# Start of the program, x transfers and idle matmuls re-ordered in a convolution and ELU-MLP kernel

## Chip, core and metric

The kernel runs on one core of a Trainium2 chip. The metric is device time in microseconds from one launch. Five engines work on their own instruction streams and meet only at semaphores: TensorE (PE; its weight loads are listed apart as PEld), VectorE (DVE), ScalarE (ACT), GpSimd (POOL) and SyncE (SP). SP, ACT and POOL also issue transfers (DMA). TensorE writes to PSUM, which here is split into a ring of three slots `H` and an accumulator `ops`.

## What is computed

The reference cut to what matters (x has 8 batches of 4096 rows of 192 channels, `weight` is 8 heads by 7 taps, `w_in` is 192 by 2048, `w_out` is 2048 by 192):

```python
w = softmax(weight, axis=-1)                      # one 7-tap filter for each head
x_pad = concat([zeros(B, 6, D), x], axis=1)       # six zero rows ahead of every batch
out[b, s, h] = sum_k w[h, k] * x_pad[b, s + k, h] # causal convolution, 24 channels a head
h = out.reshape(32768, 192) @ w_in
g = where(h > 0, h, exp(min(h, 0)) - 1)
result = g @ w_out
```

## The kernel before

**Tiling.** The 32768 rows are cut into 32 supers of 1024 rows; four supers make a batch. The 2048 hidden columns are cut into 16 pairs, each 128 columns by 1024 rows (two halves of 512). So the program has 512 pairs. A list called `order`, made ahead of the program, gives the sequence that PE, ACT and SP follow: convolution halves `("c", m)`, pairs `("h", n)` and pieces of the output product `("o", t, half, r0, r1)`.

**A pair.** PE makes the hidden values of a pair in one slot of H with six matmuls (L494). ACT takes the exponential of each half into a buffer `E` (L372), POOL clamps it to at most 1 (L308), and DVE forms max(h, e - 1) from E and from the same slot of H into `gT` (L421). Only when DVE is done is the slot free. There are three slots in turn, so a pair's matmuls wait for DVE's work on the pair three slots back (`wait_slot`, L441); a convolution half takes a slot as well. The output product of super t (L523) reads `gT` and runs on PE between the pairs of super t+1, and one piece of it ahead of that, behind pair 15 of super t. `ops` is copied out by ACT (L346) twice a super.

**The convolution.** It is a matmul of x (stationary, 24 channels of one head) with a band matrix that holds the seven taps on its diagonals (L472), 40 matmuls for half a super. The result goes through ACT (L361) to `csb`, by SP to a buffer in DRAM (`conv_slots`, L569) and back into `att` in another layout (L241). In super s the second half of the convolution of super s+1 comes behind pair 4, the first half of super s+2 behind pair 12 (`CONV_AT`).

**x.** POOL issues the loads of x for super s+2 between its clamps of super s (`X_AT`, `load_x`): at step 2 only for the first super of a batch (a small memset of the six zero rows, L257, and a transfer of the rest of window 0, L258), at step 4 windows up to 4 (L271), at step 12 windows 5 to 8 (L271). A load waits until the convolution of super s no longer needs the buffer (`s_cv`), and a step's load stands in POOL's stream ahead of that step's clamps.

**The start.** DVE makes the filter weights. SP writes a zeroed tile Tm to DRAM (`conv_band`, L544), writes the taps over its diagonal (L555), and reads the band back as `Tk`, taps and heads interleaved, heads innermost (L557). DVE and ACT each copy one half of the heads of Tk into `Tm`, which has columns innermost (L407, L326). PE runs 34 idle matmuls on a zero tile (L453, `WARM`), then the two convolution halves of super 0 out of Tm, then 24 idle matmuls, then pair 0. The second half of the convolution of super 0 is copied out by DVE (L411). POOL loads x of super 0 first, waits for the taps in DRAM (`s_band` at 32, L287), loads the first 1024 columns of w_in (L276), copies these to the upper 64 partitions (L291), waits for both convolution halves (L292), loads x of super 1, waits for `att` of super 0 (L295), and loads the other columns of w_in. w_out is loaded at step 8 of super 0 (L300).

Of the kernel before, what the change touches and what calls it, by code (L numbers as in the profile page):

```python
# [12 lines left out]
P = 128  # L13
# [3 lines left out]
HEADS = 8  # L17
# [4 lines left out]
CW = 122  # L22
# [6 lines left out]
NG3 = 2  # L29
LAG = -1  # L30
QA = 8
WARM = (34, 24)
HALF_STEPS = (10, 10, 6, 6, 10, 11, 11)

CONV_AT = ((4, 1, 1), (12, 2, 0))
EARLY_CONV = {1: (1, 0), 4: (1, 1), 12: (2, 0)}
XW = 5
X_AT = ((2, 0), (4, 1), (12, 2))
W_OUT_AT = 8

PIECES = (
# [6 lines left out]
def bass_lightweight_conv__then__act_elu_kernel(  # L48
# [84 lines left out]
    with ExitStack() as stack:  # L133
# [73 lines left out]
        NDMA_ATT = 6  # L207
        x_need, z_need, x_count, z_count = {}, {}, [0] * NXB, 0
        for s in range(NS):
            x_count[s % NXB] += 16 + 16 * (s % SPB == 0)  # L210
            z_count += s % SPB == 0
            x_need[s, 0] = x_count[s % NXB]
            x_need[s, 1] = 16 * (s // NXB + 1)
            z_need[s] = z_count
# [30 lines left out]
        @block.gpsimd  # L245
        def _gpsimd(g: bass.BassGpSimd):
            W = Waits(g)

            def load_x(s, part):
                b, t0 = s % NXB, s * SUP  # L250
                first = s % SPB == 0
                if part == 0 and not first:
                    return
                if s >= NXB:
                    W(s_cv, 2 * (s - NXB) + 2)
                if part == 0:
                    g.memset(xg[0:PAD, b, 0, :], 0.0).then_inc(s_z)  # L257
                    g.dma_start(  # L258
                        xg[PAD:P, b, 0, :], x_flat[t0 : t0 + P - PAD, :]
                    ).then_inc(s_x[b][0], 16)  # L260
                    return
                if part == 1:
                    w0, w1, row = int(first), XW, t0 - PAD + CW * first
                else:
                    w0, w1, row = XW, NWIN, t0 + SUP - P - CW * (NWIN - 1 - XW)
                src = bass.AP(
                    tensor=x_flat.tensor,
                    offset=row * D,
                    ap=[[D, P], [CW * D, w1 - w0], [1, D]],
                )  # L270
                g.dma_start(xg[:, b, w0:w1, :], src).then_inc(s_x[b][part - 1], 16)  # L271

            def load_w_in(k):
                c0, c1 = WCOLS[k]
                for j in range(3):
                    g.dma_start(  # L276
                        w_in[0:HP, j, c0:c1],
                        bass.AP(
                            tensor=moe_w_in.tensor,
                            offset=8 * j * FF + c0,  # L280
                            ap=[[CPH * FF, HEADS], [FF, 8], [1, c1 - c0]],
                        ),
                    ).then_inc(s_w[k], 16)

            for part in range(3):
                load_x(0, part)
            W(s_band, 32)  # L287
            load_w_in(0)
            W(s_w[0], 48)
            c0, c1 = WCOLS[0]  # L290
            g.dma_start(w_in[HP:P, :, c0:c1], w_in[0:HP, :, c0:c1]).then_inc(s_wdp, 16)  # L291
            W(s_cv, 2)  # L292
            for part in range(3):
                load_x(1, part)
            W(s_att[0], 16 * NDMA_ATT)  # L295
            load_w_in(1)
            for n in range(NP):
                s, i = divmod(n, NQ)
                if n == W_OUT_AT:
                    g.dma_start(  # L300
                        w_out[:, :, :], moe_w_out.rearrange("(q p) d -> p q d", p=FC)
                    ).then_inc(s_w[2], 16)
                for at, part in X_AT:
                    if at == i and s + NXB < NS:
                        load_x(s + NXB, part)
                for u in range(2):
                    W(s_exp, 2 * n + u + 1)
                    g.tensor_scalar(  # L308
                        out=E[:, n % NE, u, :],
                        in0=E[:, n % NE, u, :],  # L310
                        scalar1=1.0,
                        scalar2=0.0,
                        op0=ALU.min,
                        op1=ALU.max,
                    ).then_inc(s_clp)

        @block.scalar
        def _scalar(a):
            W = Waits(a)
            a.memzero(scr[:, 0:1]).then_inc(s_scr)  # L320
            W(s_scr, 1)
            a.activation(scr[:, 1:2], scr[:, 0:1], ACT.Exp)
            W(s_set, 2)
            a.activation(wex[:], wq2[:], ACT.Exp).then_inc(s_wex)
            W(s_band, 48)
            a.activation(  # L326
                Tm[:, HEADS // 2 :, :].rearrange("p h t -> p t h"),
                Tk[:, :, HEADS // 2 :],
                ACT.Copy,
            ).then_inc(s_tm)  # L330

            def evac(t, half):
                n_half = 2 * t + half
                W(s_mm2, n_half + 1)
                b = n_half % 2
                W(s_out[b], 32 * (n_half // 2))
                if (t, half) == last_half:
                    a.activation(  # L338
                        osb[:, b, 0, :, :].rearrange("p k d -> p (k d)"),
                        H[:, last_slot % 3, 0 : 2 * D],  # L340
                        ACT.Copy,
                    ).then_inc(s_oev)
                    W(s_od, 1)
                    out_group(a, t, half, 1)
                    return
                a.activation(  # L346
                    osb[:, b, :, :, :].rearrange("p g k d -> p g (k d)"),
                    ops[:, :, 0 : 2 * D],
                    ACT.Copy,
                ).then_inc(s_oev)  # L350

            for item in order:
                if item[0] == "c":
                    m = item[1]
                    if m == 1:
                        W(s_dw[0], 16)
                        read_att(a, W, 0, 0)
                        continue
                    W(s_cv, m + 1)
                    W(s_dw[m % 4], 16 * (m // 4))  # L360
                    a.activation(  # L361
                        csb[:, m % 4, :, :],
                        H[:, slot_of_conv[m] % 3, :].rearrange("p (b t) -> p b t", b=2),
                        ACT.Copy,
                    ).then_inc(s_ce)
                elif item[0] == "h":
                    n = item[1]
                    k = slot_of_pair[n] % 3
                    W(s_h, n + 1)
                    W(s_tt, 2 * (n - NE) + 2)  # L370
                    for u in range(2):
                        a.activation(  # L372
                            E[:, n % NE, u, :], H[:, k, GS * u : GS * (u + 1)], ACT.Exp
                        ).then_inc(s_exp)
                else:
                    _, t, half, r0, r1 = item
                    if r1 == NR:
                        evac(t, half)

        @block.vector  # L380
        def _vector(v):
# [21 lines left out]
                ALU.mult,  # L403
            ).then_inc(s_set)
            v.memset(H[:, 0:2, :], 0.0).then_inc(s_hz)
            W(s_band, 48)
            v.tensor_copy(  # L407
                Tm[:, 0 : HEADS // 2, :].rearrange("p h t -> p t h"), Tk[:, :, 0 : HEADS // 2]
            ).then_inc(s_tm)
            W(s_cv, 2)  # L410
            v.tensor_copy(  # L411
                csb[:, 1, :, :],
                H[:, slot_of_conv[1] % 3, :].rearrange("p (b t) -> p b t", b=2),
            ).then_inc(s_cd)
            for n in range(NP):
                s, q = divmod(n, NQ)
                if s >= NG3:
# [20 lines left out]
        def _tensor(pe):  # L438
# [17 lines left out]
            for item in order:  # L456
                if item[0] == "c":
                    m = item[1]
                    s, g = divmod(m, 2)
                    if m == 0:  # L460
                        W(s_tm, 2)
                        W(s_hz, 1)
                    for part in range(g + 1):
                        W(s_x[s % NXB][part], x_need[s, part])
                    W(s_z, z_need[s])
# [2 lines left out]
                    for hb in range(2):  # L468
                        for (w, c0, nc_, o) in PIECES[g]:
                            for q in range(4):  # L470
                                h = 4 * hb + q
                                ins = pe.matmul(  # L472
                                    H[SLOT * q : SLOT * q + CPH, k % 3,
                                      GS * hb + o : GS * hb + o + nc_],
                                    xg[:, s % NXB, w, CPH * h : CPH * (h + 1)],
                                    Tm[:, h, PAD + c0 : PAD + c0 + nc_],
                                    start=True,
                                    stop=True,
                                    tile_position=(0, SLOT * q),
                                )  # L480
                    ins.then_inc(s_cv)
                elif item[0] == "h":
                    n = item[1]
                    s, q = divmod(n, NQ)
                    if n == 0:
                        warm(WARM[1])
                    W(s_w[q // QA], 48)
                    W(s_wdp if q < QA else s_wd[1], 16)
                    W(s_att[s % 2], 16 * NDMA_ATT * (s // 2 + 1))
# [131 lines left out]
```

## Time and profile before

| what | value |
|---|---|
| median of 3 runs | 786.17 us (785.61 to 786.69) |
| the profiled execution | 785.69 us |
| its span, first to last instruction | 783.9 us |
| PE, POOL, ACT, DVE busy | 96%, 85%, 84%, 81% of the span |
| first matmul of pair 0 | at 28.12 us |
| first pair of super 1 | at 55.45 us |
| last instruction of L421 (DVE) ends | at 771.4 us |

The times in the profile are microseconds from the start of the span. A busy PE in the table is not a PE at its peak, since a matmul's end is modelled. In a timeline row stand start, length, engine, line, operation, destination and source, the number of instructions merged (x6), and in brackets the idle time ahead of it with the name of what ended it. A row of windows gives for a stretch its length, then busy time and number of instructions of PE, PEld, DVE, ACT and POOL, the granted clock of TensorE, the share of the DMA engines in use, and the rate.

### The profile page before, as it was taken

To read this page: it belongs to the slowest core of one execution; us is meant where nothing else is said; L and a number is where in the kernel's file an instruction comes from. 1 tells how busy PE (TensorE), PEld (TensorE's weight loads), DVE (VectorE), ACT (ScalarE), POOL (GpSimd) and SP (SyncE) were. 2 spreads that over 40 slices of the span, in tenths; PEclk is the share of its full clock that TensorE was granted. 3 is DMA by queue.
4 is the path that set the end of the run, shared out by engine and by line. 5 is a ranking of instruction groups with operands and counts; after the bars stand their busy time and mean duration, and the time that the engine had idled before them with its cause. 6 is when DMAs were issued, how large, how long until landed. Compare 5 with 4: busy or idle time off the path is not lost.

```text
span 783.9 us, 32275 instructions
## 1 busy us (share of the span) xinstructions
PE 751.1 (96%) x13882; PEld 514.9 (66%) x13882; DVE 638.0 (81%) x1035; ACT 658.4 (84%) x1156; POOL 663.3 (85%) x1116
## 2 busy tenths in 40 slices
PE   8479999999999999999999999999999999999997
PEld 3136666766666666666676666666667666666766
DVE  3378888888888888888888888888888888888893
ACT  2478888898889888888888888988888988898883
POOL 3488988988888898898898888889889889888882
PEclk9889999999999999999999999999999999999999
DMA  6674344344344435434444433443443444444212
GB/s 106 113 120 88 83 109 86 90 109 104 76 104 92 101 87 112 93 79 111 83 91 109 109 81 93 83 111 89 110 92 84 107 83 94 104 111 83 77 42 63
DMA packets 108031, 73.71 MB, mean 94 GB/s; under 512 B 45520, under 2 KB 106960, under 8 KB 107888
## 3 DMA queue, kind: packets, MB, share of 16 engines
q1 hardware_dynamic: 66344, 55.14, 22.2%
q0 software_dynamic: 41056, 16.11, 19.3%
q8 instruction: 109, 1.79, 0.9%
q10 hardware_dynamic: 488, 0.39, 0.2%
q14 instruction: 34, 0.28, 0.1%
HBM read 44.31 MB, written 42.24 MB: 110 GB/s over the span
## 4 chain that ended last, share of the span: by engine, by line
PE 41%; POOL 38%; DVE 11%; ACT 5%; DMA 2%; issue 2%; SPq 0%
POOL E L308 32%; PE H L494 24%; PE ops L523 16%; DVE gT L421 10%; POOL xg L271 6%; ACT E L372 5%; DMA conv_slots<-csb 1%; PE H L523 1%; POOL xg L258 0%; DMA conv_band<-wprb 0%; PE H L472 0%; DMA wq<-in_weight_dram 0%; DMA Tk<-conv_band 0%; ACT Tm L326 0%; DMA att<-conv_slots 0%
## 5 line engine op out<-in xcount | busy, mean ns | idle before, releaser
L421 DVE SCALAR_TENSOR_TENSOR gT<-E,H 128x512 f16<-128x512 f32 x1024 | 631.1, 682 | 123.1 <-POOL E L308 122.5
L308 POOL TENSOR_SCALAR E<-E 128x512 f32<-128x512 f32 x1024 | 602.0, 614 | 85.9 <-ACT E L372 77.4
L372 ACT ACTIVATE E<-H 128x512 f32<-128x512 f32 x1024 | 548.7, 597 | 97.8 <-PE H L494 81.4
L494 PE MATMUL H<-att,w_in 64*128 64x512 bf16 x3072 | 409.2, 379 | 19.6 <-DVE gT L421 10.1
L523 PE MATMUL ops<-w_out,gT 64*128 64x192 f16 x8064 | 414.7, 243 | 0.9 <-DVE gT L421 0.9
L523 PEld LDWEIGHTS ops<-w_out,gT 64*128 64x128 f16 x8064 | 342.7, 94 | 109.9 <-DVE gT L421 1.1
L494 PEld LDWEIGHTS H<-att,w_in 64*128 64x128 bf16 x3072 | 130.5, 94 | 125.0 <-DVE gT L421 30.8
L361 ACT ACTIVATE csb<-H 128x1024 bf16<-128x1024 f32 x63 | 64.5, 1023 | 5.4 <-PE H L472 5.2
L346 ACT ACTIVATE osb<-ops 128x768 f32<-128x768 f32 x63 | 51.5, 818 | 5.1 <-PE ops L523 5.1
L271 POOL DMA_DIRECT2D xg<-in_x_dram x64 | 53.1, 830 | 0.4 <-PE H L472 0.4
L472 PE MATMUL H<-Tm,xg 128*24 128x122 bf16 (+1 forms) x2560 | 43.1, 213 | 7.4 <-DVE gT L421 5.0
L472 PEld LDWEIGHTS H<-Tm,xg 128*24 128x24 bf16 x2560 | 33.5, 94 | 19.4 <-issue 16.5
L453 PE MATMUL ops<-zw 128*128 128x512 bf16 x58 | 16.5, 454 | 1.2 <-DVE zw L383 1.2
L276 POOL DMA_DIRECT2D w_in<-in_moe_w_in_dram x6 | 3.5, 584 | 15.7 <-DMA att<-conv_slots 10.3
L453 PEld LDWEIGHTS ops<-zw 128*128 128x128 bf16 x58 | 6.4, 113 | 10.6 <-issue 5.1
L326 ACT ACTIVATE Tm<-Tk 128x544 bf16<-128x544 bf16 x1 | 2.5, 2542 | 7.0 <-DMA Tk<-conv_band 7.0
L432 DVE COPY osb<-H 128x384 f32<-128x384 f32 x1 | 0.6, 558 | 8.9 <-PE H L523 8.9
L523 PE MATMUL H<-w_out,gT 64*128 64x192 f16 x128 | 5.6, 243 | 0.1
L523 PEld LDWEIGHTS H<-w_out,gT 64*128 64x128 f16 x128 | 5.2, 94 | 0.3 <-PE H L523 0.3
L258 POOL DMA_DIRECT2D xg<-in_x_dram x8 | 4.8, 602 | 0.3 <-issue 0.3
L407 DVE COPY Tm<-Tk 128x544 bf16<-128x544 bf16 x1 | 1.3, 1335 | 3.9 <-DMA Tk<-conv_band 3.9
L338 ACT ACTIVATE osb<-H 128x384 f32<-128x384 f32 x1 | 0.5, 490 | 4.7 <-PE H L523 4.7
(20 smaller groups left out, 11.3 us busy)
## 6 DMA issues: line engine op xcount, KB each, us to landing
out_dram<-osb SPq DMA_DIRECT2D x127, 192.0 KB, 2.4
conv_slots<-csb SPq DMA_DIRECT2D x64, 256.0 KB, 3.2
att<-conv_slots SPq DMA_DIRECT2D x189, 64.0 KB
xg<-in_x_dram POOLq DMA_DIRECT2D x40, 192.0 KB, 3.8
xg<-in_x_dram POOLq DMA_DIRECT2D x24, 240.0 KB, 4.5
w_in<-in_moe_w_in_dram POOLq DMA_DIRECT2D x6, 128.0 KB, 3.8
w_out<-in_moe_w_out_dram POOLq DMA_DIRECT2D x1, 768.0 KB, 8.8
w_in<-w_in POOLq DMA_DIRECT2D x1, 384.0 KB, 4.6
```

The source lines that it names most:

```text
L258: g.dma_start(xg[PAD:P, b, 0, :], x_flat[t0 : t0 + P - PAD, :]).then_inc(s_x[b][0], 16)
L271: g.dma_start(xg[:, b, w0:w1, :], src).then_inc(s_x[b][part - 1], 16)
L276: g.dma_start(w_in[0:HP, j, c0:c1], bass.AP(tensor=moe_w_in.tensor, offset=8 * j * FF + c0, ap=[[CPH * FF, HEADS], [FF, 8], [1, c1 - c0]], ...
L308: g.tensor_scalar(out=E[:, n % NE, u, :], in0=E[:, n % NE, u, :], scalar1=1.0, scalar2=0.0, op0=ALU.min, op1=ALU.max,).then_inc(s_clp)
L346: a.activation(osb[:, b, :, :, :].rearrange("p g k d -> p g (k d)"), ops[:, :, 0 : 2 * D], ACT.Copy,).then_inc(s_oev)
L361: a.activation(csb[:, m % 4, :, :], H[:, slot_of_conv[m] % 3, :].rearrange("p (b t) -> p b t", b=2), ACT.Copy,).then_inc(s_ce)
L372: a.activation(E[:, n % NE, u, :], H[:, k, GS * u : GS * (u + 1)], ACT.Exp).then_inc(s_exp)
L421: v.scalar_tensor_tensor(out=gT[:, s % NG3, q, u, :], in0=E[:, n % NE, u, :], scalar=1.0, in1=H[:, slot_of_pair[n] % 3, GS * u : GS * (u + ...
L453: pe.matmul(ops[:, 0, :], zw[:, 0:P], zw[:], start=True, stop=True)
L472: ins = pe.matmul(H[SLOT * q : SLOT * q + CPH, k % 3, GS * hb + o : GS * hb + o + nc_], xg[:, s % NXB, w, CPH * h : CPH * (h + 1)], Tm[:, ...
L494: ins = pe.matmul(H[:, k % 3, GS * r : GS * (r + 1)], w_in[HP * r : HP * (r + 1), j, FC * q : FC * (q + 1)], att[HP * r : HP * (r + 1), s ...
L523: ins = pe.matmul(acc[:, g, D * kb : D * (kb + 1)], gT[HP * rt : HP * (rt + 1), t % NG3, q, g, t0 : t0 + P], w_out[HP * rt : HP * (rt + 1) ...
```

## The change

Four edits, made together:

- Both convolution halves of super 0 read the band out of `Tk`, where the columns of one head are 8 elements (16 bytes) apart, and wait for Tk alone. `Tm` is now filled by one copy on DVE for all heads, behind DVE's copy of the second convolution half; ACT has no part in it. The third half (m = 2) waits for Tm.
- POOL no longer waits for the taps ahead of w_in, nor for the convolution ahead of x of super 1: the order is x of super 0, the first part of w_in, x of super 1, then the copy of w_in to the upper partitions.
- x of a batch's first super is loaded like that of any other: five windows with the six rows ahead of them, which belong to the batch before. At step 10 POOL waits for this transfer and writes zeros over the six rows. Only super 0 keeps the old way. The two loads for super s+2 stand at steps 5 and 13 instead of 4 and 12.
- In super 0, ahead of each of pairs 1 to 14, PE runs two idle matmuls.

```diff
-WARM = (34, 24)
+WARM = (34, 24, 2)
-X_AT = ((2, 0), (4, 1), (12, 2))
+X_AT = ((5, 1), (10, 0), (13, 2))
...
-            x_count[s % NXB] += 16 + 16 * (s % SPB == 0)
+            x_count[s % NXB] += 16 + 16 * (s == 0)
...
+                if part == 0:
+                    if s:
+                        W(s_x[b][0], x_need[s, 0])
+                    g.memset(xg[0:PAD, b, 0, :], 0.0).then_inc(s_z)
+                    if s == 0:
+                        g.dma_start(
+                            xg[PAD:P, b, 0, :], x_flat[0 : P - PAD, :]
+                        ).then_inc(s_x[b][0], 16)
+                    return
                 if s >= NXB:
                     W(s_cv, 2 * (s - NXB) + 2)
-                if part == 0:
-                    g.memset(xg[0:PAD, b, 0, :], 0.0).then_inc(s_z)
-                    g.dma_start(
-                        xg[PAD:P, b, 0, :], x_flat[t0 : t0 + P - PAD, :]
-                    ).then_inc(s_x[b][0], 16)
-                    return
                 if part == 1:
-                    w0, w1, row = int(first), XW, t0 - PAD + CW * first
+                    w0, w1, row = int(s == 0), XW, t0 - PAD + CW * (s == 0)
...
-            W(s_band, 32)
             load_w_in(0)
+            for part in range(3):
+                load_x(1, part)
             W(s_w[0], 48)
             c0, c1 = WCOLS[0]
             g.dma_start(w_in[HP:P, :, c0:c1], w_in[0:HP, :, c0:c1]).then_inc(s_wdp, 16)
-            W(s_cv, 2)
-            for part in range(3):
-                load_x(1, part)
...
-            W(s_band, 48)
-            a.activation(
-                Tm[:, HEADS // 2 :, :].rearrange("p h t -> p t h"),
-                Tk[:, :, HEADS // 2 :],
-                ACT.Copy,
-            ).then_inc(s_tm)
...
-            W(s_band, 48)
-            v.tensor_copy(
-                Tm[:, 0 : HEADS // 2, :].rearrange("p h t -> p t h"), Tk[:, :, 0 : HEADS // 2]
-            ).then_inc(s_tm)
             W(s_cv, 2)
             v.tensor_copy(
                 csb[:, 1, :, :],
                 H[:, slot_of_conv[1] % 3, :].rearrange("p (b t) -> p b t", b=2),
             ).then_inc(s_cd)
+            v.tensor_copy(Tm[:, :, :].rearrange("p h t -> p t h"), Tk[:]).then_inc(s_tm)
...
                     if m == 0:
-                        W(s_tm, 2)
+                        W(s_band, 48)
                         W(s_hz, 1)
+                    if m == 2:
+                        W(s_tm, 1)
...
-                                    Tm[:, h, PAD + c0 : PAD + c0 + nc_],
+                                    Tm[:, h, PAD + c0 : PAD + c0 + nc_]
+                                    if s
+                                    else Tk[:, PAD + c0 : PAD + c0 + nc_, h],
...
                     if n == 0:
                         warm(WARM[1])
+                    elif n < NQ - 1:
+                        warm(WARM[2])
```

## The prediction

> **What bounds the kernel now.** I read the page first, for the busy shares and the costliest groups.
>
> ```profile
> span 783.9 us, 32275 instructions
> PE 751.1 (96%) x13882; PEld 514.9 (66%) x13882; DVE 638.0 (81%) x1035; ACT 658.4 (84%) x1156; POOL 663.3 (85%) x1116
> ...
> L326 ACT ACTIVATE Tm<-Tk 128x544 bf16<-128x544 bf16 x1 | 2.5, 2542 | 7.0 <-DMA Tk<-conv_band 7.0
> ...
> L407 DVE COPY Tm<-Tk 128x544 bf16<-128x544 bf16 x1 | 1.3, 1335 | 3.9 <-DMA Tk<-conv_band 3.9
> ```
>
> PE is nearly full on average, so work taken from other engines pays only where PE waits for them. That is the case in two places: the start, where PE has no input, and two short waits in every super. The waits of PE's weight loads from 60 us on show the second:
>
> ```profile
> PEld H L494 <- DVE gT L421: 19.4, 58, 0.4
> ```
>
> 58 waits are two in each of 29 supers, 0.33 us each. The timelines of POOL and PE show where they come from and what a super costs without them. Super 29 still loads x, super 30 has no x left to load but still has the convolution half at step 4:
>
> ```profile
> 709.18 0.89 POOL L271 DMA_DIRECT2D xg<-in_x_dram  x1
> ...
> 711.78 1.19 POOL L308 TENSOR_SCALAR E<-E 128x512 f32<-128x512 f32 x2 [0.47 <-ACT E L372]
> ...
> 732.47 1.19 POOL L308 TENSOR_SCALAR E<-E 128x512 f32<-128x512 f32 x2 [0.28 <-ACT E L372]
> 734.73 1.19 POOL L308 TENSOR_SCALAR E<-E 128x512 f32<-128x512 f32 x2 [1.06 <-ACT E L372]
> ```
>
> ```profile
> 707.99 0.81 PE L494 MATMUL H<-att,w_in 64*128 64x512 bf16 x6
> ...
> 719.52 0.81 PE L494 MATMUL H<-att,w_in 64*128 64x512 bf16 x6
> ...
> 730.94 0.81 PE L494 MATMUL H<-att,w_in 64*128 64x512 bf16 x6
> ...
> 742.27 0.81 PE L494 MATMUL H<-att,w_in 64*128 64x512 bf16 x6
> ```
>
> The four PE rows are pairs 4 and 12 of super 29 and the same of super 30. In super 29 POOL issues a transfer (0.89 us) ahead of the clamps of pair 4. They come late, DVE frees pair 4's slot late, and pair 6, which needs that slot because a convolution half took one in between, stands. From pair 4 to pair 12 this half takes 11.53 us; the next half, with the step 12 transfer, 11.42. In super 30, with the convolution but no transfer, 11.33. The row at 734.73 also shows that POOL then waits 1.06 us for ACT ahead of pair 5.
>
> For the start I read the chain of waits in order of time:
>
> ```profile
> 0.76 2.96 DMA wq<-in_weight_dram
> ...
> 5.50 3.22 DMA conv_band<-wprb
> ...
> 8.73 2.69 DMA Tk<-conv_band
> ...
> 11.44 2.55 ACT Tm L326
> ...
> 14.04 1.94 PE H L472 x75
> ...
> 16.00 1.24 DVE csb L411
> ...
> 17.25 6.92 DMA conv_slots<-csb
> ...
> 25.59 2.39 DMA att<-conv_slots
> ```
>
> All of it is serial, and pair 0 follows on PE at 28.12. Two items stand out: the copy into Tm, and 6.92 us for writing a result whose median elsewhere is 3.2 us (page's DMA table):
>
> ```profile
> conv_slots<-csb SPq DMA_DIRECT2D x64, 256.0 KB, 3.2
> ```
>
> It was issued at 17.25, while x of super 1 and the copy of w_in were under way.
>
> **The change part by part.**
>
> **Start.** Conv 0 may begin when Tk has landed (11.42) instead of at 14.04: -2.6 us. The 34 idle matmuls end at 11.64, so PE is free. DVE's single copy into Tm comes behind its csb copy; two halves at 1335 ns make 2.7 us, while DVE has nothing to do until pair 0, so it costs nothing; uncovered it would be those 2.7.
>
> Tk itself may land later, since the loads of w_in and of x of super 1 now run beside the writing and reading of the band. Lower bound 0: the taps took 3.22 us beside x of super 0, whose queue held nearly all of the DMA engines (second row: its packets, MB and share from 6 to 8.7 us), hardly more than the 2.96 of the first, quiet load.
>
> ```profile
> q0 software_dynamic: 836, 0.31, 97.2%
> ```
>
> Upper bound +3.7, what the conv_slots write lost in such company (6.92 against 3.2). I take +0.8, nearer the small end, since the taps' write went out on the same SP queue beside engines as busy as they will be for Tk. The Trainium skill, in "DMA: Bandwidth & Descriptors", section "Queues, rings and completion order", says that a DMA engine takes turns between the queues that have work, packet by packet. By that rule Tk's moving part would about double and the start would gain about 1 us less than I sum here; the taps' row shows little of it.
>
> The convolution reads Tk at a step of 16 bytes. No matmul here does that. Read densely at full clock 40 matmuls take 0.65:
>
> ```profile
> 720.67 0.65 PE L472 MATMUL H<-Tm,xg 128*24 128x122 bf16 x40
> ```
>
> so 80 take 1.3 at the least. The strided copies give a price for scattered elements: DVE 1335 ns for 544 is 2.45 ns each, against 1.24 us for 1024 or 1.21 in the csb copy, twice; ACT's 2542 for 544 is 4.67, 3.9 times. That makes 2.6 or 5.0 us in place of 1.94. I take 2.6, the smaller ratio, since both copies also scatter their writes, which the matmuls don't: +0.7, bounds -0.6 and +3.1.
>
> Then csb (unchanged) and its write. Beside it, w_in no longer waits for the taps in DRAM (8.72) nor x for the convolution (15.98), so both should be mostly done by then: 3.6 instead of 6.92, -3.3, bounds -3.7 (the median) and 0. The copy of w_in to the upper partitions is now behind x in POOL's queue; I expect it landed some 5 us ahead of pair 0. Sum of the start: -2.6 + 0.8 + 0.7 - 3.3 = **-4.4**.
>
> **Super 0.** From pair 0 to the first pair of super 1 it takes 27.33 us:
>
> ```profile
> 28.12 2.75 PE L494 MATMUL H<-att,w_in 64*128 64x512 bf16 x12 [6.16 <-DMA att<-conv_slots]
> ...
> 46.30 0.82 PE L494 MATMUL H<-att,w_in 64*128 64x512 bf16 x6 [1.53 <-DVE gT L421]
> ...
> 51.80 2.74 PE L494 MATMUL H<-att,w_in 64*128 64x512 bf16 x12 [0.45 <-DVE gT L421]
> ...
> 55.45 0.81 PE L494 MATMUL H<-att,w_in 64*128 64x512 bf16 x6
> ```
>
> ```profile
> 36.24 0.94 POOL L271 DMA_DIRECT2D xg<-in_x_dram  x1
> ...
> 48.97 0.79 POOL L271 DMA_DIRECT2D xg<-in_x_dram  x1
> ```
>
> The two transfers stand in POOL's serial path here; one step later they fall into its wait for ACT: -0.9 and -0.7. The clock, by the windows (length, busy time by engine, granted clock):
>
> ```profile
> 20.80:24.20 3.40, 1.16 (x6) 0.31 (x4) 0.00 (x0) 0.00 (x0) 0.00 (x0) 1.00 1.21 222
> ...
> 44.70:48.10 3.40, 1.50 (x14) 0.42 (x12) 3.15 (x6) 2.03 (x4) 3.35 (x7) 1.00 1.15 124
> 48.10:51.50 3.40, 2.80 (x48) 1.17 (x46) 2.77 (x5) 2.37 (x5) 2.86 (x5) 0.50 1.32 190
> ```
>
> After a stretch in which PE was busy 1.50 of 3.40 us the clock is halved. From 51.80 two pairs and 20 output matmuls then take 3.65 us; at full clock the same sequence takes 2.13, from 99.88 to 102.01:
>
> ```profile
> 99.88 1.47 PE L494 MATMUL H<-att,w_in 64*128 64x512 bf16 x12
> ...
> 102.01 0.81 PE L494 MATMUL H<-att,w_in 64*128 64x512 bf16 x6
> ```
>
> Two idle matmuls ahead of each pair, 0.51 us by the next row, come at least twice in such a stretch and make 2.5 of 3.4 of it; the clock should hold: -1.5. Their price, 24 in 6.08 us:
>
> ```profile
> 15.88 6.08 PE L453 MATMUL ops<-zw 128*128 128x512 bf16 x24
> ```
>
> That is 0.51 us for two, 7.1 for 28. Mostly PE would stand waiting for DVE there (up to 1.53 us, row at 46.30), so they cost nothing; five pairs follow straight on another and could lose 0.51 each, 2.5, if ACT and POOL were not behind them with work. At pair 1 the clock is likely still halved (PE is again idle for some 4 us ahead of pair 0); there the pair of idle matmuls takes 3.65/2.13 times 0.51 = 0.87 on a path with no cover. Sum -0.9 - 0.7 - 1.5 + 0.9 = **-2.2**, bounds -3.8 (pair 0 warm too) and +1.7 (clock lost, five pairs late).
>
> The Trainium skill's "TensorE: Matmul & The Clock Gate", Part 1, lets the clock fall after an idle window of about 3.4 us. By that rule the waits of at most 1.53 us would not have halved it, and the idle matmuls would bring nothing; the halved clock after the 44.70 window goes against it.
>
> **Supers 1 to 29.** The issue of 0.89 moves behind the clamps of pair 4 (and 12), into the 1.06 us that POOL waits there. So each half should take super 30's 11.33: 11.53 + 11.42 - 22.66 = 0.29, times 29 = **-8.4**. That is less than the 19.4 of the waits, because DVE's pairs 6 to 8 are then next late: POOL runs without a gap from pair 6 on and pairs 9 to 11 wait a little for its slots. Bounds: the whole 19.4, and nothing. The transfers land in time: issued at step 5, they land 5.6 us later at the worst, and the convolution that reads them is seven pairs on.
>
> ```profile
> DMA to landing us min/median/max: 3.4/4.0/5.6
> ```
>
> **Batches.** Seven supers also issue the memset and the extra transfer, and one of them takes 102.01 - 78.38 = 23.63 instead of 22.95, +0.68:
>
> ```profile
> 78.38 0.81 PE L494 MATMUL H<-att,w_in 64*128 64x512 bf16 x6
> ```
>
> ```profile
> 82.51 0.25 POOL L257 MEMSET xg<- 6x192 bf16 x1
> 82.71 0.59 POOL L258 DMA_DIRECT2D xg<-in_x_dram  x1
> ```
>
> Afterwards only the memset's 0.25 remains, at step 10. POOL's wait ahead of it is over by then (five pairs are over 6 us, the landing 5.6). Behind it queue the clamps of pairs 10 to 12; POOL's 0.28 us wait at pair 12 takes most of it up. I keep 0.2, bounds 0 and 0.4: 0.48 times 7 = **-3.4**.
>
> Sum: -4.4 - 2.2 - 8.4 - 3.4 = -18.4. The profiled execution took 785.69 (span 783.9 and 1.8 around it), 0.48 below the median: 767.3, and **767.8** against the runs.
>
> **The rivals.**
>
> *The stall vanishes whole.* All 19.4 us come back, 11.0 more: 756.8. Against it: super 30's residual waits.
>
> *The stall only moves.* The transfers delay pair 5's slot and so pair 8 as they did pair 4's and 6: 8.4 is not gained, 776.2. For it: the wait ahead of pair 5 was only 0.47 us in super 29. Against: 0.47 came after a late pair 4.
>
> *The start is dear.* Tk +3.7, conv 5.0, the csb write as slow as before: 2.9 + 2.4 + 3.3 = 8.6 lost, 776.4. It needs three bad ends at once.
>
> *The idle matmuls don't hold the clock*, as the skill's rule would also have it: 1.5 lost, 769.3.
>
> *Slower.* At steps 5 and 13 POOL's wait is not there when the issue comes, since PE, no longer stalled, brings pair 5 to ACT sooner. If half of 0.84 is then charged to each half, a super takes 22.66 + 0.84 = 23.50, 0.55 above before; times 29 is +16.0, less the other 10.0: 792.2. It decides from 0.35 a super on, 0.32 charged a half. Against it: with no stall at all super 30 showed 1.06 us of room for 0.89.
>
> **How the numbers follow.** Forecast 0.60 with its own range 763 to 772; whole stall gone 0.08; stall moves 0.13; dear start 0.08; clock not held 0.05; slower 0.06. The range of 760 to 776.5 leaves out the first and last of the rivals and the far ends. A measurement here tells 0.2% (1.6 us) from no change. Faster 0.92; within 0.2% 0.02 (a moved stall and a dear start together, 784.8); slower 0.06.
>
> **What would show it.** Right: a super of 22.7 us, batch supers 0.2 above; no wait of 0.3 us for DVE at pairs 6 and 14; the issue at steps 5 and 13 with almost no POOL wait behind it; pair 0 near 23.7; Tk landing near 12.2; clock 1.00 at the end of super 0. Wrong: supers of 22.9 or more, the strided conv far above 2.6 us, or pair 0 later than 26.

## The result and the profile after

The changed kernel takes 768.1 us (median, 767.72 to 768.94) beside 785.89 of the kernel before (785.6 to 786.69). The ratio is 0.9774, with an interval of 0.9757 to 0.979. The profiled execution took 768.94 us with a span of 767.1, and before 785.69 with 783.9, so the terms below add up to 16.75 us, while the medians differ by 17.8.

| stretch (us) | before | after | predicted | measured |
|---|---|---|---|---|
| start to pair 0 | 28.12 | 27.41 | -4.4 | -0.71 |
| super 0 | 27.33 | 24.72 | -2.2 | -2.61 |
| supers 1 to 29 | 670.21 | 656.66 | -11.8 | -13.55 |
| super 30 | 21.84 | 21.96 | 0 | +0.12 |
| from super 31 on, to the end of the span | 36.4 | 36.35 | 0 | -0.05 |

Each stretch ends at the first matmul of pair 0 of the next super in PE's timeline. The forecast of 767.8 was met by a sum in which the start fell short by 3.7 us. The supers gave 2.2 more than predicted, and the three other runs of the changed kernel were 0.84 to 1.22 us faster than the profiled one.

From the page after, the span, the busy shares, the first convolution's matmuls, and the writes of `conv_slots` (number, KB each, median us to landing):

```profile
span 767.1 us, 32323 instructions
...
PE 752.3 (98%) x13910; PEld 515.0 (67%) x13910; DVE 638.7 (83%) x1035; ACT 645.2 (84%) x1155; POOL 661.8 (86%) x1109
...
L466 PE MATMUL H<-Tk,xg 128*24 128x122 bf16 (+1 forms) x80 | 3.9, 363 | 4.7 <-DMA Tk<-conv_band 4.7
...
conv_slots<-csb SPq DMA_DIRECT2D x64, 256.0 KB, 2.5
```

**The steady part.** What PE's weight loads waited for from 60 us on, after (total, times, longest):

```profile
PEld ops L521 <- ACT osb L341: 10.9, 62, 0.2
PEld H L466 <- issue: 9.1, 58, 0.2
```

The 58 waits for DVE are gone. New are 62 short ones, two in a super, for ACT's copy of the output product. They are waits of the weight loads, which overlap matmuls, so they aren't lost time one for one. The stretch from 60 to 760 us shows what PE itself has left (length, then busy PE, PEld, DVE, ACT, POOL, clock, DMA share, GB/s), first before, then after:

```profile
60.00:760.00 700.00, 689.89 (x13060) 480.38 (x13056) 598.06 (x972) 620.12 (x1093) 620.80 (x1045) 1.00 0.42 94
```

```profile
60.00:760.00 700.00, 699.05 (x13276) 490.44 (x13274) 605.17 (x984) 615.54 (x1104) 625.74 (x1048) 1.00 0.43 95
```

PE stands 0.95 us in 700 where it stood 10.11, and gets 216 more matmuls done in them. It now sets the pace alone. PE's timeline after: pair 4 of super 29 and of super 30, and then one pair of an early super in which POOL zeroes rows for a batch, with the same pair a super later:

```profile
691.54 0.81 PE L492 MATMUL H<-att,w_in 64*128 64x512 bf16 x6
...
714.20 0.81 PE L492 MATMUL H<-att,w_in 64*128 64x512 bf16 x6
```

```profile
76.13 0.82 PE L492 MATMUL H<-att,w_in 64*128 64x512 bf16 x6
...
98.79 0.82 PE L492 MATMUL H<-att,w_in 64*128 64x512 bf16 x6
```

Both take 22.66 us. A batch costs nothing any more. POOL's timeline after shows where the issues and the memset stand:

```profile
90.14 0.25 POOL L258 MEMSET xg<- 6x192 bf16 x1
...
92.87 1.19 POOL L310 TENSOR_SCALAR E<-E 128x512 f32<-128x512 f32 x2 [0.18 <-ACT E L367]
...
693.07 1.19 POOL L310 TENSOR_SCALAR E<-E 128x512 f32<-128x512 f32 x2 [0.28 <-ACT E L367]
694.21 0.89 POOL L275 DMA_DIRECT2D xg<-in_x_dram  x1
695.35 1.18 POOL L310 TENSOR_SCALAR E<-E 128x512 f32<-128x512 f32 x2 [0.25 <-ACT E L367]
```

Behind the issue POOL still waits 0.25 us for ACT, and two pairs after the memset 0.18, so neither seems to delay a clamp that PE would miss.

**The start.** The chain of waits after (start, length, what):

```profile
5.49 5.64 DMA conv_band<-wprb
...
11.15 4.94 DMA Tk<-conv_band
...
16.13 3.89 PE H L466 x76
...
21.29 2.17 DMA conv_slots<-csb
...
24.88 2.40 DMA att<-conv_slots
```

The taps take 5.64 us instead of 3.22, Tk 4.94 instead of 2.69, the convolution 3.89 instead of 1.94. The copy of 2.6 us is gone, and the write of `conv_slots` takes 2.17 instead of 6.92. So 6.6 us are lost to 7.3 gained. Super 0 on PE, from its first pair to the first of super 1, with 0.16 us lost to the landing of w_out:

```profile
27.41 0.82 PE L492 MATMUL H<-att,w_in 64*128 64x512 bf16 x6 [1.97 <-DMA att<-conv_slots]
...
51.30 1.00 PE L521 MATMUL ops<-w_out,gT 64*128 64x192 f16 x20 [0.16 <-DMA w_out<-in_moe_w_out_dram]
52.13 0.81 PE L492 MATMUL H<-att,w_in 64*128 64x512 bf16 x6
```

### The profile page after: what moved, and what is told of

Same layout as the page of the kernel before. It is cut to its first block, busy times and chain, and to the rows that moved or that the text cites. A ratio compares the mean times of both kernels' runs of the same rounds, so it can differ in the third digit from the quotient of the medians.

```text
span 767.1 us, 32323 instructions
## 1 busy us (share of the span) xinstructions
PE 752.3 (98%) x13910; PEld 515.0 (67%) x13910; DVE 638.7 (83%) x1035; ACT 645.2 (84%) x1155; POOL 661.8 (86%) x1109
## 4 chain that ended last, share of the span: by engine, by line
PE 93%; DMA 4%; DVE 1%; POOL 1%; ACT 0%; issue 0%; SPq 0%; POOLq 0%
PE ops L521 44%; PE H L492 44%; PE H L466 5%; DMA w_out<-in_moe_w_out_dram 1%; DMA conv_band<-wprb 1%; PE H L521 1%; DVE gT L413 1%; DMA Tk<-conv_band 1%; POOL E L310 0%; DMA wq<-in_weight_dram 0%; DMA att<-conv_slots 0%; ACT E L367 0%; DMA conv_slots<-csb 0%; POOL w_in L280 0%; PE ops L445 0%
## 5 line engine op out<-in xcount | busy, mean ns | idle before, releaser
L356 ACT ACTIVATE csb<-H 128x1024 bf16<-128x1024 f32 x63 | 64.5, 1023 | 13.7 <-PE H L466 13.7
L275 POOL DMA_DIRECT2D xg<-in_x_dram x64 | 53.8, 842 | 0.4 <-issue 0.4
L466 PE MATMUL H<-Tm,xg 128*24 128x122 bf16 (+1 forms) x2480 | 40.7, 209 | 0.6 <-DVE gT L413 0.6
L466 PEld LDWEIGHTS H<-Tm,xg 128*24 128x24 bf16 x2480 | 31.3, 92 | 11.2 <-issue 11.2
L445 PE MATMUL ops<-zw 128*128 128x512 bf16 x86 | 24.2, 421 | 1.2 <-DVE zw L378 1.2
L466 PE MATMUL H<-Tk,xg 128*24 128x122 bf16 (+1 forms) x80 | 3.9, 363 | 4.7 <-DMA Tk<-conv_band 4.7
L466 PEld LDWEIGHTS H<-Tk,xg 128*24 128x24 bf16 x80 | 2.3, 117 | 6.4 <-DMA Tk<-conv_band 5.2
```

The lines of the kernel that those rows point to most:

```text
L356: a.activation(csb[:, m % 4, :, :], H[:, slot_of_conv[m] % 3, :].rearrange("p (b t) -> p b t", b=2), ACT.Copy,).then_inc(s_ce)
L445: pe.matmul(ops[:, 0, :], zw[:, 0:P], zw[:], start=True, stop=True)
L466: ins = pe.matmul(H[SLOT * q : SLOT * q + CPH, k % 3, GS * hb + o : GS * hb + o + nc_], xg[:, s % NXB, w, CPH * h : CPH * (h + 1)], Tm[:, ...
```

## The experiments

The theory after the result: the steady gain comes from where the two issues stand, the batch gain from the one transfer less, and the start lost its gain to POOL's loads ahead of the band. Each edit is shown against the changed kernel. Times taken on different chips are compared by their ratio to the kernel before, measured on the same chip.

### The issues back at steps 4 and 12

```diff
-X_AT = ((5, 1), (10, 0), (13, 2))
+X_AT = ((4, 1), (10, 0), (12, 2))
```

> The two x loads back at steps 4 and 12, the batch memset still at step 10, all else as changed. Theory: the issue ahead of pairs 4 and 12 makes the wait of PE for DVE; a super goes from 22.65 back to 22.95, 29 times 0.30 = 8.7, and super 0 gets 0.5 to 1.5 longer: 777.5 to 778.5. Rival: the gain of 13.5 us in supers 1 to 29 came from the batch loads or the new start; then 768 to 769.

780.49 us, ratio 0.9922 (0.9907 to 0.9937). Its weight loads' waits from 60 us on:

```profile
PEld H L492 <- DVE gT L413: 20.5, 58, 0.6
...
PEld ops L521 <- ACT osb L341: 0.7, 4, 0.2
```

The 58 waits for DVE are back, two in a super, and those for ACT's output copy are gone. Supers 1 to 29 take 667.17 us, 10.5 more than in the changed kernel. Super 0 takes 25.81, 1.1 more. One step for two issues is thus worth the larger part of the whole change. The time is 2 us above the expected 778.5: the seven batch supers take 23.11 to 23.36 us here, 0.16 to 0.41 more than the others, so with the issues at the old steps the memset at step 10 isn't free.

### The batch load of before

```diff
-X_AT = ((5, 1), (10, 0), (13, 2))
+X_AT = ((2, 0), (5, 1), (13, 2))
...
-            x_count[s % NXB] += 16 + 16 * (s == 0)
+            x_count[s % NXB] += 16 + 16 * (s % SPB == 0)
...
-                if part == 0:
-
-                    if s:
-                        W(s_x[b][0], x_need[s, 0])
-                    g.memset(xg[0:PAD, b, 0, :], 0.0).then_inc(s_z)
-                    if s == 0:
-                        g.dma_start(
-                            xg[PAD:P, b, 0, :], x_flat[0 : P - PAD, :]
-                        ).then_inc(s_x[b][0], 16)
-                    return
                 if s >= NXB:
                     W(s_cv, 2 * (s - NXB) + 2)
+                if part == 0:
+                    g.memset(xg[0:PAD, b, 0, :], 0.0).then_inc(s_z)
+                    g.dma_start(
+                        xg[PAD:P, b, 0, :], x_flat[t0 : t0 + P - PAD, :]
+                    ).then_inc(s_x[b][0], 16)
+                    return
                 if part == 1:
-                    w0, w1, row = int(s == 0), XW, t0 - PAD + CW * (s == 0)
+                    w0, w1, row = int(first), XW, t0 - PAD + CW * first
```

> The batch's first super loaded as before (memset and an extra transfer at step 2, four windows), the other two loads at steps 5 and 13. Theory: each of seven supers pays 0.6 to 0.7 us again, others stay at 22.65: 772.3 to 773. Rival: with the other loads out of the way POOL's waits at pairs 4 and 5 take up the extra issue; then 768 to 769.

772.87 us, ratio 0.9821 (0.9803 to 0.9838). Supers 1 to 29 take 660.63, 3.97 more than in the changed kernel, which is 0.57 for each of the seven supers. The waits of its weight loads, and a place in PE's timeline of such a super:

```profile
PEld H L462 <- issue: 12.7, 58, 0.7
```

```profile
81.70 0.66 PE L462 MATMUL H<-Tm,xg 128*24 128x24 bf16 x40 [0.48 <-DVE gT L409]
```

The loss is in one place: the convolution half behind pair 4 finds its slot still held by DVE, three pairs after POOL spent 0.84 us at step 2 on the memset and the issue. In the kernel before the same group of waits held 13.4 us.

```profile
PEld H L472 <- issue: 13.4, 59, 0.7
```

### No idle matmuls in super 0

```diff
-WARM = (34, 24, 2)
+WARM = (34, 24, 0)
```

> No idle matmuls ahead of pairs 1 to 14, all else as changed. Theory: the clock falls to half in super 0 as in the kernel before, pair 0 of super 1 comes 1 to 2 us later: 769 to 770. Rival, by the Trainium skill's TensorE: Matmul & The Clock Gate, Part 1 (a fall only after an idle window): no fall without a gap of about 3.4 us, so 767.5 to 768.2, and the idle matmuls are useless or cost.

768.65 us, ratio 0.9773 (0.9758 to 0.9788): the same as with them. Windows of its super 0 (columns as above):

```profile
28.00:31.40 3.40, 1.37 (x46) 0.63 (x43) 2.23 (x4) 2.37 (x5) 2.77 (x5) 1.00 0.76 116
31.40:34.90 3.50, 3.19 (x40) 1.25 (x44) 1.90 (x4) 2.55 (x5) 2.20 (x4) 0.51 0.46 97
...
41.70:45.10 3.40, 1.64 (x12) 0.42 (x12) 2.32 (x5) 2.02 (x4) 3.37 (x6) 1.00 0.70 70
```

The clock falls once, behind a window with PE busy 1.37 of 3.40, and not at the end of the super, where PE is busy 1.64 of 3.40. Super 0 takes 24.96 us against 24.72. Together with the run at steps 4 and 12 this makes a table of four: 27.33 with neither edit (the kernel before, with its own start), 25.81 with the idle matmuls alone, 24.96 with the moved issues alone, 24.72 with both. Beside the idle matmuls, the moved issues are worth 1.1. The 2.4 from the kernel before to this one holds the new start too: the 12 matmuls of pairs 0 and 1 took 2.75 us there at a granted clock near 0.5 and take 1.47 here. How much each gave is not shown. The idle matmuls are worth 0.24, which can't be told from nothing. They do hold the clock, which was granted at 1.00 all through super 0 of the changed kernel. But there they set PE's pace, a pair every 1.29 us, while the pairs here follow at 1.19 where DVE keeps up.

The fall at 31.4 follows a longest wait of 1.96 us:

```profile
30.51 0.82 PE L492 MATMUL H<-att,w_in 64*128 64x512 bf16 x6 [1.96 <-DVE gT L413]
```

The Trainium skill's "TensorE: Matmul & The Clock Gate", Part 1, asks for an idle window of about 3.4 us before the clock falls. That the idle matmuls bring nothing agrees with what the prediction worked out from that rule, but not for its reason: the clock fell without them, behind a wait of 1.96 us, which doesn't agree with the rule as the prediction read it.

### The load order of before

```diff
             for part in range(3):
                 load_x(0, part)
+            W(s_band, 32)
             load_w_in(0)
-            for part in range(3):
-                load_x(1, part)
...
             g.dma_start(w_in[HP:P, :, c0:c1], w_in[0:HP, :, c0:c1]).then_inc(s_wdp, 16)
+            W(s_cv, 2)
+            for part in range(3):
+                load_x(1, part)
```

> POOL's order at the start as before (w_in waits for the taps, x of super 1 for the convolution), all else as changed. Theory: w_in and x of super 1 beside the band held up the taps (5.64 us) and Tk (4.94). Then here the taps take about 3.2, Tk lands near 11.4, the convolution starts near 11.5 and takes some 2 us at full clock, the csb write is slow again (6 to 7 us), pair 0 near 25.5, the time near 766.3. Rival: the two band transfers were late for another reason; then Tk still lands near 16, the csb write is slow on top of it, pair 0 is near 32 and the time near 773.

769.57 us, ratio 0.9794 (0.9778 to 0.9811). Its chain:

```profile
5.52 3.29 DMA conv_band<-wprb
...
8.83 2.71 DMA Tk<-conv_band
...
11.58 3.87 PE H L468 x76
...
16.73 5.66 DMA conv_slots<-csb
...
26.29 1.47 PE H L494 x6
```

The taps and Tk are back at 3.29 and 2.71, so the loads ahead of them were what delayed them. The `conv_slots` write is back at 5.66 beside x of super 1. Pair 0 comes 1.1 us earlier, but the clock was granted at 0.5 from 23.19 to 30.01, super 0 takes 25.80, and super 1 begins at 52.09 against 52.13. The expected time of 766.3 was missed for two reasons. The convolution was expected to take some 2 us at full clock; the clock was granted at 1.00 from 11.5 to 15.5 us, and it took 3.87 all the same. And an earlier pair 0 isn't an earlier super 1.

### x of super 1 ahead of w_in

```diff
+            for part in range(3):
+                load_x(1, part)
+            W(s_band, 32)
             load_w_in(0)
-            for part in range(3):
-                load_x(1, part)
```

> x of super 1 straight behind x of super 0, then the wait for the taps, then w_in and its copy. Theory A: what held up the band were w_in's long packets (2 KB); with x's short ones (384 B) the taps take 3.5 and Tk 3.2, Tk lands near 12.3, pair 0 near 24, time near 764.8. Theory B: any load queued beside the band holds it up for as long as it lasts; then the taps still take 5 us or more, Tk lands at 15 or later, and the time is 767 to 769.

768.7 us, ratio 0.9786 (0.9769 to 0.9803). Its chain:

```profile
5.51 5.47 DMA conv_band<-wprb
...
11.00 2.69 DMA Tk<-conv_band
...
13.73 3.88 PE H L467 x79
```

x of super 1 holds the taps about as long as w_in did, which is Theory B. Tk, issued when those loads had all but landed, takes 2.69 and lands at 13.69, and not at 15 or later as that theory had it. Pair 0 comes at 26.34 and super 1 at 51.97, 0.16 earlier than in the changed kernel. In these runs the taps land with the loads that were queued ahead of them, whichever they are. What POOL's queue moved between the issue of the taps and their landing (packets, MB, share), in the changed kernel from 5.5 to 11.2 us, and in the kernel with half of the heads dense, below, from 5.4 to 7:

```profile
q0 software_dynamic: 2042, 1.00, 134.5%
```

```profile
q0 software_dynamic: 314, 0.11, 60.7%
```

The same write of 14 KB took 5.64 us with 1.00 MB of POOL's queue beside it and 1.4 with 0.11 MB. Why so small a write doesn't pass the loads is not shown.

### Conv 0 out of the dense Tm again

```diff
+            W(s_band, 48)
+            a.activation(
+                Tm[:, HEADS // 2 :, :].rearrange("p h t -> p t h"),
+                Tk[:, :, HEADS // 2 :],
+                ACT.Copy,
+            ).then_inc(s_tm)
...
-                                    Tm[:, h, PAD + c0 : PAD + c0 + nc_]
-                                    if s
-                                    else Tk[:, PAD + c0 : PAD + c0 + nc_, h],
+                                    Tm[:, h, PAD + c0 : PAD + c0 + nc_],
```

DVE copies the other half of the heads, as before, and PE waits for both copies.

> The first two convolution halves read Tm, filled by ACT and DVE halves as before; all else as changed. Theory: reading at a step of 16 bytes doubles the matmuls (3.87 us against 1.94 dense, both at half clock), so the step gives back 1.9 of the 2.6 that the copy cost: 768.7, conv 1.9 us after a Tm copy of 2.5. Rival: the 3.87 us are due to the clock and not to the step; then the conv here stays near 3.9 and the time is near 770.7.

770.94 us, ratio 0.9811 (0.9794 to 0.9828). Its chain:

```profile
16.10 2.55 ACT Tm L328
...
18.69 1.94 PE H L474 x67
```

The dense convolution takes 1.94 us at half clock, 1.95 less than out of Tk, behind a copy of 2.55. Reading the band in place thus gains 0.6 us on this chain. The theory was right on this step, and 2.2 us short on the time. Pair 0 came at 29.05 and super 1 at 54.62, 2.5 later than in the changed kernel, which is more than the copy explains: the reading of `att` took 3.42 there instead of 2.40, and super 0 took 0.85 longer, with the clock granted at 0.50 from 29.57 to 32.98.

### Idle matmuls up to the first convolution

```diff
-WARM = (34, 24, 2)
+WARM = (57, 24, 2)
```

> 57 idle matmuls at the start instead of 34, so that PE is busy until Tk lands near 16.1. Theory: the strided convolution scales with the clock; at full clock it takes 2.0 instead of 3.87 us, pair 0 comes 1.5 to 1.9 us earlier, time near 766.4. Rival: the step is bound by the reading from SBUF and not by the clock; the convolution still takes 3.5 us or more, time 767.7 to 768.5.

769.28 us, ratio 0.9794 (0.9777 to 0.981). The question was whether the 3.89 us are the strided reading or the clock, which in the changed kernel was granted at 0.50 during the convolution. The chain, and the window of the convolution:

```profile
16.46 3.82 PE H L466 x77
```

```profile
16.40:20.30 3.90, 3.86 (x81) 2.26 (x82) 0.00 (x0) 1.02 (x1) 0.00 (x0) 1.00 0.01 4
```

At full clock it takes 3.82. So it is the strided operand and not the clock: 48 ns a matmul, with either clock, against 1.3 us for 80 dense matmuls at full clock. The total says nothing on this: Tk was issued at 11.44 and landed 3.6 us later, so the idle matmuls held the convolution up for 1.4 us.

### The changed kernel once more

> The changed kernel unaltered, as the measure for the other three: 768 to 769 on the chip of the first result.

769.09 us, ratio 0.9778 (0.9764 to 0.9791), with pair 0 at 27.31 and super 1 at 51.90. The three kernels that share its start (with steps 4 and 12, with the old batch load, without idle matmuls) had Tk at 3.96, 3.43 and 3.75 us and pair 0 at 26.82, 26.91 and 26.50, so a difference under 1 us at pair 0 is no finding by itself.

### x of super 1 behind the convolution's write

```diff
+            W(s_band, 32)
             load_w_in(0)
-            for part in range(3):
-                load_x(1, part)
...
+            W(s_dw[1], 16)
+            for part in range(3):
+                load_x(1, part)
```

Here and in the next kernel 32 idle matmuls stand ahead of pair 0 instead of 24.

> w_in again behind the taps, x of super 1 behind the landing of the second convolution half's write, 32 instead of 24 idle matmuls ahead of pair 0. Theory: a transfer lands right behind the loads that stand in POOL's queue when it is issued, so with none there the taps take 3.3, Tk 2.7 (lands 11.5), and the csb write 2.2 to 3.5 (5.66 with the old order); pair 0 near 23.2 instead of 27.4, and with the clock held super 0 takes 24.7 to 25: time 764 to 765. Rival: pair 0 is early but super 0 is longer by as much (clock halved at its start, or w_out's landing ahead of super 1), so the time stays at 767.5 to 768.5.

769.42 us, ratio 0.9779 (0.9766 to 0.9793). From the chain, and the window ahead of and in pair 0:

```profile
21.73 4.66 DMA att<-conv_slots
```

```profile
24.40:27.80 3.40, 1.27 (x6) 0.33 (x6) 0.00 (x0) 0.00 (x0) 1.12 (x2) 0.50 0.59 84
```

x of super 1 no longer meets the write but the reading of `att` behind it, which goes from 2.40 to 4.66. The taps and Tk came as expected, at 3.02 and 2.60, but pair 0 at 26.53 instead of 23.2, with the clock at 0.50, and super 1 at 52.37. The expected gain wasn't there.

### The same with w_out earlier

```diff
-W_OUT_AT = 8
+W_OUT_AT = 5
```

One idle matmul, not two, stands ahead of each pair of super 0.

> The kernel a_x1_behind_csb with w_out loaded at step 5 and one idle matmul ahead of each pair instead of two. Theory: with two, PE needs 1.29 us a pair against POOL's 1.19, with one 1.08, so POOL sets the pace and super 0 gets 1 to 1.3 us shorter if w_out is there in time: 1 us faster than a_x1_behind_csb. Rival: one idle matmul doesn't hold the clock; then a half-clock window costs 1 us or more and nothing is gained.

769.38 us, ratio 0.9782 (0.9768 to 0.9795). w_out now stands ahead of x of super 2 in POOL's queue, and PE waited for that x:

```profile
47.91 0.65 PE L468 MATMUL H<-Tm,xg 128*24 128x122 bf16 x40 [1.79 <-DMA xg<-in_x_dram]
```

Super 0 took 27.55 us. The wait for w_out was exchanged for a longer one, and the rival came true as well: behind this wait the clock was granted at 0.50 from 48.93 to 52.34.

### Half of the heads dense, x of super 0 in two parts

Beside the edits of the last two kernels, with 30 idle matmuls ahead of the convolution instead of 34:

```diff
-            for part in range(3):
+            for part in range(2):
                 load_x(0, part)
+            W(s_band, 32)
+            load_x(0, 2)
...
-                    for hb in range(2):
+                    for hb in (1, 0) if m == 0 else (0, 1):
+                        if m == 0 and hb == 0:
+                            W(s_tm, 1)
...
-                                    if s
+                                    if s or hb == 0
```

DVE copies heads 0 to 3 into Tm while PE reads heads 4 to 7 out of Tk.

> The kernel b_w_out_at_5_one_idle with the second part of x of super 0 behind the taps and with heads 0 to 3 of the first two convolution halves read from Tm (DVE copies these 4 heads while PE reads heads 4 to 7 at a step out of Tk). Theory: taps land 1 us earlier (7.7), Tk near 10.4, the convolution 2.6 to 3.0 us instead of 3.87: pair 0 1.8 us earlier, time 1.5 to 2 us below b_w_out_at_5_one_idle. Rival: the taps don't land earlier with half of x ahead of them; then 0.5 to 0.9 us.

767.17 us (765.42 to 769.13), ratio 0.9753 (0.9735 to 0.9771). Chain and one row of PE's timeline:

```profile
10.71 2.45 PE H L477 x76
...
18.03 5.32 DMA att<-conv_slots
...
23.49 0.92 PE H L503 x6
...
48.63 0.82 PE H L503 x6
```

```profile
44.10 0.65 PE L477 MATMUL H<-Tm,xg 128*24 128x122 bf16 x40 [1.44 <-DMA xg<-in_x_dram]
```

The taps land at 6.94, Tk at 9.67, and super 1 begins 3.3 us earlier than in the repeat of the changed kernel, in a profiled execution that is 3.34 faster (765.42 against 768.76). The medians, taken on the same chip, differ by 1.9 us, and the intervals of the ratios overlap: it is at best a little faster. Why its runs spread over 3.7 us is not settled; only the fastest of them has a trace.

### w_out behind x of super 2

```diff
-W_OUT_AT = 5
+W_OUT_AT = 6
```

This is against the kernel just above, with 44 idle matmuls ahead of pair 0 instead of 32.

> The kernel c_half_dense with w_out loaded at step 6, behind x of super 2 in POOL's queue instead of ahead of it (at step 5 the convolution half behind pair 12 waited 1.44 us for x, which had 9.95 us from issue to landing), and 44 instead of 32 idle matmuls ahead of pair 0. Theory: x of super 2 lands in 5 us again and that wait is gone, and PE is not idle long enough ahead of pair 0 to be halved: super 0 takes 23.3 to 23.8 instead of 25.14, ratio to the kernel before 0.972 to 0.974. Rival: w_out's own landing, or att of super 1 beside it, takes the wait's place; then 0.975 as for c_half_dense.

767.11 us, ratio 0.9759 (0.974 to 0.9777). The wait for x is gone, but the rival came true: PE waits for `att` of super 1 instead, whose data are written to DRAM beside w_out.

```profile
50.28 0.82 PE L503 MATMUL H<-att,w_in 64*128 64x512 bf16 x6 [1.03 <-DMA att<-conv_slots]
```

```profile
37.58 7.43 DMA conv_slots<-csb
```

Nor did the 44 idle matmuls hold the clock, which was granted at 0.50 from 26.02 to 29.43.

## Why the prediction was right, and where not

**Supers 1 to 29, right in size, not in what is late next.** Predicted 22.66 us a super by reading super 30's halves, measured 22.66. With the issues back at steps 4 and 12 the 58 waits return, which shows the cause. The prediction said that of the 19.4 us of waits only 8.4 come back because DVE's pairs 6 to 8 are then late and pairs 9 to 11 wait for slots. The trace shows none of that: PE is busy 699.05 of 700 us and no pair waits for DVE. The rest of the 19.4 did not come back because PE itself is the bound. The trace before held this: from 730.94 to 742.27, the half that the forecast was read from, PE was busy 11.33 of 11.33 us, and in the half with an issue (from 707.99) 11.39 of 11.53. The half showed PE's own pace, which is why its length held though the reason given for it didn't.

**Batches, underestimated.** The step "I keep 0.2" was 0: a batch super takes 22.66. The memset's 0.25 us delays no clamp that PE waits for, since the next wait of POOL for ACT, 0.18, is still there behind it; with the issues at steps 4 and 12 it did cost 0.16 to 0.41. With the old load 0.57 a batch comes back, of the 0.68 that were read from the trace of before.

**The start, wrong.** The term "I take +0.8" for Tk failed. It read the taps' 3.22 us beside x of super 0 as little delay, and took it as the price for a busy queue. It was the time that POOL's loads ahead of it needed to land. With w_in and x of super 1 also ahead, taps and Tk together took 10.6 us instead of 5.9, +4.7, which is beyond the bound of 3.7; Tk landed at 16.09 where 12.2 was forecast. With the old load order they take 6.0. The rule of the Trainium skill that the prediction weighed ("DMA: Bandwidth & Descriptors", section "Queues, rings and completion order": engines take turns between queues by packets) was one by which, as it worked out, Tk's moving part would about double. Tk went from 2.69 to 4.94 in the profiled run and to between 3.43 and 4.80 in six others with the same order of loads, mostly nearer to that than to my reading. For the taps the turns are not what the runs show: their 144 packets landed with the 2042 of the other queue.

The strided convolution was mis-sized in the same direction: +0.7 predicted, +1.95 measured, within the bounds. The ratio was taken from DVE's strided copy (about twice); it is 2.9 times the dense 1.3 us at full clock, between DVE's twice and ACT's 3.9 times. (That 3.9 sets ACT's strided copy against DVE's dense one; against ACT's own dense copy, 1023 ns for 1024 elements, it is 4.7.) The write of `conv_slots` went the other way, -4.75 instead of -3.3; POOL's queue moved nothing beside it from 21.3 to 23.5 us. The rival "the start is dear" thus came true in one of its three ends. Two of the signs that were named for a wrong forecast appeared, pair 0 later than 26 and a convolution far above 2.6 us.

**Super 0, right in sum, not by its terms.** -2.2 predicted, -2.61 measured. The -1.5 for the clock held by idle matmuls fell, as in the rival "the idle matmuls don't hold the clock", but for another reason: they hold it, and take about as much of PE's time as the one fall without them costs. The moved issues, costed at 0.9 and 0.7, bring 1.1 beside the idle matmuls; without these, the 2.4 against the kernel before can't be parted from the new start. The +0.9 at pair 1 for a halved clock didn't come: the clock was full there.

**Slower.** Its mechanism, POOL's wait gone when the issue comes, isn't there: 0.25 us of wait are left behind the issue, and supers got shorter.

So the total came out by errors that cancel: the start 3.7 short, the batches, the steady part and super 0 2.2 over, a profiled execution 0.84 above its median, and 0.48 that the forecast had added for the median of before. That 768.1 came within 0.3 of 767.8 is luck; the size of the steady part is not.

## What to carry to other kernels

Cost an issue on an engine's stream by the wait that it delays or fills: one step of difference for two issues of 0.8 to 0.9 us in each super was worth 11 to 12 us here, and a stage without that issue told the size in advance. Before a small transfer on a critical path is costed, list what other queues have pending when it is issued, and price it by their landing, not by its bytes. A gain ahead of a stage counts only when the end of that stage moves: six other versions of the start had pair 0 earlier, by 0.9 (which the same start also varies by) to 3.9 us, and only one of them had super 1 begin over 2 us earlier.

## What the runs showed of the hardware that I had not expected

A 14 KB write on SP's queue took 1.4, 3.22 and 5.64 us, with 0.11, 0.35 and 1.00 MB of POOL's queue moved meanwhile. Matmuls whose moving operand has a step of 16 bytes took 48 ns each, 3.82 to 3.91 us for 80, the same at granted clocks of 1.00 and 0.50, while the dense ones took 1.94 at 0.50. The granted clock fell behind windows of 3.40 us in which PE was busy 1.37 us (without idle matmuls) and 1.50 us (the kernel before), with no wait above 1.96 us in either, and did not fall behind one with 1.64. A threshold on the busy share of a window would fit these three, but not two others: behind 1.50 of 3.50 us (without idle matmuls, from 24.5) the clock held, and behind 1.62 of 3.41 (w_out at step 5, from 45.52) it fell. What decides stays open; no run was made for it.
